# Batch 0's q and k: cast by GpSimd and transposed as bf16, with a new instruction order

## The chip, the cores and the metric

The kernel runs on one core of one Trainium2 chip. The metric is the device time of one execution in microseconds. The core has five engines that run side by side, each through its own list of instructions in order: TensorE (PE, with its weight loads shown apart as PEld), VectorE (DVE), ScalarE (ACT), GpSimd (POOL) and SyncE (SP), which here only issues DMAs. They wait for each other through semaphores.

## The reference

Eight batches, eight heads, 576 positions, head size 64. Linear attention with a feature map of 2 x 128 features, and then a gated linear unit with a causal convolution as gate:

```python
def phi(x):
    proj = np.einsum('bhsd,df->bhsf', x, w_phi)
    proj = proj - np.max(np.abs(proj), axis=-1, keepdims=True)
    return np.concatenate([np.exp(proj), np.exp(-proj)], axis=-1)
q_p, k_p = (phi(q), phi(k))
kv = np.einsum('bhsf,bhsd->bhfd', k_p, v)
z = np.sum(k_p, axis=2)
num = np.einsum('bhsf,bhfd->bhsd', q_p, kv)
den = np.einsum('bhsf,bhf->bhs', q_p, z)[..., None] + 1e-06
x = num / den            # then [batch, seq, heads * 64]
gate = sigmoid(causal convolution of x with conv_w, 5 taps)
out = (gate * (x @ w_val)) @ w_out
```

Inputs and output are fp32.

## The kernel before

Each batch goes through the same stages. q and k of a batch are seen as 18 blocks of 128 x 128; they are taken in five units `u` of 4, 4, 4, 4 and 2 blocks. Inside one batch:

- q and k are brought to SBUF and transposed to `qT` and `kT` (128 x 2304, bf16). For batches 2 to 7 a DMA transposes them (`xpose`). For batch 1 PE transposes bf16 data that a casting DMA has brought (`tp16`, evicted from PSUM by `tc16`). For batch 0 the fp32 data comes by nine plain loads of SyncE (`load32`: four pieces of k, five of q), PE transposes it as fp32 (`tp32`, L544) and DVE or ACT evicts it with a cast to bf16 (`tc32`, L550 and L552).
- `kp` and `qm` (L585) project a unit, 128 features by two row halves, into two PSUM banks. DVE takes the largest magnitudes (`kmax`, `qmax`, L593, tiles MK and MQP), ACT takes exp of plus and minus the projection of k (`kexp`, L603, tile KTIL).
- `ek` (ACT, L612) and `vs` (POOL, L618 and L619) scale v; `st` (PE, L628) sums k's features against v; `kv` evicts that (tile KV, by DVE at L636 or ACT at L640).
- The maxima of q are transposed and spread (`mqt`, `mqr`, `rx`: POOL at L690 or DVE at L693); `qp` (PE, L701 and L706) projects q again with the maxima taken off in the same banks; `qexp` (ACT, L714 and L717) gives QTIL and QTT.
- `num` (PE, L727 and L734), `nrm` (DVE, L745 and L748), `xtp` and `xtc` (transpose of x and its eviction), then `gate` (PE, L789), `tanh` (ACT, L793), `val` (PE, L799), `gv` (DVE, L805), `out` (PE, L821 and L825), `oev` (eviction) and `odma` (store).

The fp32 data of batch 0, `XN32`, lies in the memory of KTIL's second buffer, which batch 1's `kexp` writes. The three GV buffers are first written by `gv` of batches 0 to 2.

`build` writes all these steps as tasks with their dependencies. The order in which they are issued is a table, ORDER, of task numbers, found by a search outside the kernel; each engine runs its tasks in that order. FLEX names the engine of each task that may run on two, and BANKS the PSUM banks. The durations in the calls of `A(...)` served that search and issue nothing. WARM and ZERO are tables of filler for PE: `warm` multiplies ones by ones into a bank that is free (L499), `zero` adds products of zeros to a bank that has just been written (L512 and L505). In ZERO the entry `37:78:7` means: ahead of the 37th step, seven times, into the banks of task 78.

POOL also issues the casting loads of later batches' q and k. A tiny copy (`hold`, L517), which reads a piece of batch 0's q, stands ahead of batch 1's loads on POOL's queue, so that these do not start while batch 0's still run.

Of the kernel before, what the change touches and what calls it, by code (L numbers as in the profile page):

```python
# [14 lines left out]
BF16 = mybir.dt.bfloat16  # L15
# [19 lines left out]
WARM = "62:6:1 83:1:1 89:7:2 136:7:1 143:7:1"  # L35
ZERO = "37:78:7 63:82:5 77:36:1 103:107:1 120:101:1 128:217:8 146:225:1 157:194:4 160:202:1 177:317:6 191:348:1 197:243:2 199:243:2 213:329:1"
# [41 lines left out]
)  # L78
FLEX = (
    "DAAAAAADAAADDPPPPDDDDAADDDDDDDDDDDDDAAADAAAADDDDAAADDDAADAAADDADAADDDDADDDDADDDDDDAADADDAAAAAA"  # L80
)
BANKS = (
    "703736230700145452323232301670167671423236723010167601235442301014545450101366056467560145674501014545010167676701450145"
    "454567201237670123016767674567777356723236723234545230167232323236767454501545234362367010123234545445223014545016767676"
    "701012301450123016745012016736401234523674545455572301454523456723232301012323674523016723234670142201016745456701012165"
    "670145670101230167012301016723236767456702367726012323012323016746464450101670167012367674567234523234545012367015767234"
    "5010167452326322345670145670101674545012345012367452345010127452301014545670101765"
)


# [18 lines left out]
def dve(n, ov=0.075):  # L109
    return n / 960.0 + ov  # L110


def act(n):
    return n * 0.000833 + 0.067
# [794 lines left out]
```

## Time and profile before

| | |
|---|---|
| median of 3 runs | 218.67 us (217.57 to 219.39) |
| profiled execution, own time | 216.94 us |
| its span, first to last instruction | 215.2 us |
| instructions | 9031 |
| granted TensorE clock | 0.995 |
| PE busy / DVE / ACT / POOL | 195.4 / 170.0 / 180.5 / 132.9 us |

A page of the profile has the busy time of each engine, the span in 40 slices of 5.4 us with the busy share of each engine in tenths, the chain of work that ended last, and groups of instructions. A group's line reads: line of the kernel, engine, operation, what it writes and reads with the shapes, and count; then busy microseconds in total and the mean nanoseconds of one; then the idle time of that engine just before them and who ended it. In a timeline row stand the start, the length, the engine and the operation, and in brackets the idle time before it. "issue" as a releaser is time in which the engine waited for nothing that the profile shows. Matmuls overlap, so lengths of single ones add to more than their busy time.

### The profile page before, as it was taken

The page shows a single profiled execution, that of the slowest core. Times are in us where ns is not written, and L with a number is a line of the kernel's source. Part 1 is how long each engine was busy: PE and PEld are TensorE (multiplying, and loading weights), DVE is VectorE, ACT ScalarE, POOL GpSimd, SP SyncE. Part 2 cuts the span into 40 slices and gives each one's busy share as a digit, 9 for nine tenths or more (in the row PEclk, how much of TensorE's full clock was granted, in tenths as well). Part 3 has the DMA queues.
Part 4 walks back from the last instruction along what each step waited for, and adds up shares of the span by engine and source line. Part 5 has one row for each costly group of instructions (what it writes and reads, how often), then busy time and mean ns, then how long its engine had stood idle before and what let it go on. Part 6 is the DMA issues. An engine that isn't in the chain of part 4 may idle for free.

```text
span 215.2 us, 9031 instructions
## 1 busy us (share of the span) xinstructions
PE 195.4 (91%) x3948; PEld 138.4 (64%) x3948; DVE 170.0 (79%) x258; ACT 180.5 (84%) x267; POOL 132.9 (62%) x172
## 2 busy tenths in 40 slices
PE   2969788778999999999999999999999999999990
PEld 2745466566665776677767677568757766687640
DVE  3399789989599978999799978998699897654510
ACT  3799999999999899999899997999988988634351
POOL 3156999896893749953997099903992879210000
PEclk9999999999999999999999999999999999999997
DMA  6999989999999698969998978979953265773165
GB/s 195 371 223 199 297 175 192 231 195 198 138 241 251 113 172 241 264 104 188 216 303 155 116 146 259 187 154 202 280 179 84 67 160 128 97 165 88 49 205 188
DMA packets 49874, 39.89 MB, mean 185 GB/s; under 512 B 34149, under 2 KB 39461, under 8 KB 49834
## 3 DMA queue, kind: packets, MB, share of 16 engines
q1 hardware_dynamic: 43616, 28.65, 58.1%
q0 software_dynamic: 6032, 10.49, 26.5%
q8 instruction: 31, 0.51, 0.9%
q10 hardware_dynamic: 186, 0.17, 0.3%
q14 instruction: 9, 0.07, 0.1%
HBM read 30.45 MB, written 9.44 MB: 185 GB/s over the span
## 4 chain that ended last, share of the span: by engine, by line
PE 55%; ACT 22%; DVE 15%; issue 4%; DMA 1%; DVEq 0%; ACTq 0%
PE PS L799 11%; PE PS L821 10%; PE PS L789 9%; ACT QTIL L714 9%; ACT KTIL L603 9%; DVE MQP L593 5%; PE PS L727 5%; PE PS L585 4%; PE PS L628 4%; DVE MK L593 4%; PE PS L701 2%; PE PS L825 2%; PE PS L706 2%; PE PS L544 2%; DVE XN L748 2%
## 5 line engine op out<-in xcount | busy, mean ns | idle before, releaser
L603 ACT ACTIVATE KTIL<-PS 128x1024 bf16<-128x1024 f32 (+1 forms) x80 | 72.1, 965 | 4.0 <-PE PS L585 2.0
L618 POOL TENSOR_TENSOR VT<-VN,EK 128x1152 bf16<-128x1152 f32 x32 | 67.9, 2121 | 4.5 <-ACT EK L612 4.4
L714 ACT ACTIVATE QTIL<-PS 128x1024 bf16<-128x1024 f32 x64 | 62.6, 1047 | 2.3 <-PE PS L706 1.5
L690 POOL TENSOR_TENSOR RX<-MQR,ident 128x512 bf16<-128x512 bf16 (+1 forms) x39 | 36.6, 962 | 35.1 <-DVE MQR L678 32.4
L593 DVE TENSOR_REDUCE MK<-PS 128x8 f32<-128x1024 f32 (+1 forms) x40 | 44.3, 1113 | 3.4 <-PE PS L585 1.6
L593 DVE TENSOR_REDUCE MQP<-PS 128x8 bf16<-128x1024 f32 (+1 forms) x40 | 43.5, 1112 | 3.0 <-PE PS L585 2.3
L799 PE MATMUL PS<-XT,WV 128*128 128x288 bf16 x256 | 34.8, 286 | 0.2 <-DVE GV L805 0.2
L805 DVE SCALAR_TENSOR_TENSOR GV<-TH,PS 128x576 bf16<-128x576 bf16 x32 | 23.8, 752 | 10.4 <-PE PS L799 4.7
L821 PE MATMUL PS<-WOUT,GV 128*128 128x512 bf16 x128 | 31.3, 380 | 0.0
L799 PEld LDWEIGHTS <-WV 128*128 128x128 bf16 x256 | 23.8, 98 | 7.8 <-issue 1.4
L793 ACT ACTIVATE TH<-PS 128x576 bf16<-128x576 f32 x32 | 20.5, 667 | 8.8 <-PE PS L789 8.2
L789 PE MATMUL PS<-XT,GW 64*64 64x288 bf16 x640 | 23.6, 285 | 0.9 <-DVE RCP L745 0.4
L628 PE MATMUL PS<-VT,KTIL 64*128 64x65 bf16 x1152 | 23.1, 191 | 0.1
L748 DVE TENSOR_TENSOR XN<-PS,RCP 128x512 bf16<-128x512 f32 x32 | 22.1, 691 | 1.1
L727 PEld LDWEIGHTS <-QTIL 128*128 128x128 bf16 x512 | 18.3, 97 | 6.4 <-issue 4.1
L628 PEld LDWEIGHTS <-KTIL 64*128 64x128 bf16 x1152 | 20.7, 95 | 2.6 <-issue 1.5
L727 PE MATMUL PS<-KV,QTIL 128*128 128x65 bf16 x512 | 20.3, 193 | 0.3 <-DVE MQP L593 0.2
L789 PEld LDWEIGHTS <-GW 64*64 64x64 bf16 x640 | 18.0, 106 | 3.8 <-issue 1.6
L642 ACT ACTIVATE OUTS<-PS 128x512 f32<-128x512 f32 x22 | 13.7, 627 | 7.3 <-PE PS L821 6.1
L821 PEld LDWEIGHTS <-GV 128*128 128x128 bf16 x128 | 11.1, 98 | 11.3 <-issue 0.6
L585 PE MATMUL PS<-W,qT 64*128 64x128 bf16 x288 | 14.9, 217 | 3.8 <-ACT qT L552 0.9
L585 PEld LDWEIGHTS <-qT 64*128 64x128 bf16 x288 | 10.6, 94 | 10.4 <-issue 5.1
(82 smaller groups left out, 234.5 us busy)
## 6 DMA issues: line engine op xcount, KB each, us to landing
out_dram<-OUTS SPq DMA_DIRECT2D x32, 256.0 KB, 3.4
VN<-in_v_dram SPq DMA_DIRECT2D x7, 1152.0 KB, 7.2
KQN<-in_q_dram POOLq DMA_DIRECT2D x6, 576.0 KB, 8.0
KQN<-in_k_dram POOLq DMA_DIRECT2D x6, 576.0 KB, 9.1
KTIL<-in_k_dram SPq DMA_DIRECT2D x4, 288.0 KB, 3.7
VN<-in_v_dram POOLq DMA_DIRECT2D x1, 1152.0 KB, 12.3
KTIL<-in_q_dram SPq DMA_DIRECT2D x4, 256.0 KB, 4.9
out_dram<-OUTS SPq DMA_DIRECT2D x14, 64.0 KB, 2.4
```

The costliest lines, as they stand in the source:

```text
L585: nc.tensor.matmul(self.PS[:, t.grp.banks[par], i * P:(i + 1) * P], X[rows, (c0 + i) * P:(c0 + i + 1) * P], self.W2[rows, :], start=True, ...
L593: self.nc.vector.tensor_reduce(o, self.two(t.grp, n * P).rearrange("p a (c f) -> p a c f", f=F), AX.X, ALU.max, apply_absolute_value=True)
L603: self.nc.scalar.activation(self.KTIL[b % 2][:, s, c0:c0 + n, :, :].rearrange("p c a f -> p a c f"), self.two(t.grp, n * P).rearrange("p a ...
L618: nc.gpsimd.tensor_tensor(self.VT[g][:, s, :, 0:D], self.VN[b % 2][:, NC * g:NC * g + NC, :], e.to_broadcast([P, NC, D]), ALU.mult)
L628: nc.tensor.matmul(self.PS[:, t.grp.banks[ab], (s * 2 + x) * E1:(s * 2 + x + 1) * E1], self.KTIL[b % 2][rows, s, J // 2, J % 2, :], self.V ...
L690: self.nc.gpsimd.tensor_tensor(o, *wide(self.MQR[self.mq(b, u)][:, :], self.ident2), ALU.mult)
L714: self.nc.scalar.activation(o, i, AF.Exp, scale=1.0 - 2.0 * s)
L727: nc.tensor.matmul(self.PS[:, t.grp.banks[h // 4], (h % 4) * E1:(h % 4 + 1) * E1], Q[:, s, c % 2, h, (c // 2) * P:(c // 2 + 1) * P], self. ...
L748: nc.vector.tensor_tensor(o.rearrange("p (g h) d -> p g h d", g=ng), n[:, :, :, 0:D], rc.unsqueeze(3).to_broadcast([P, ng, 4, D]), ALU.mult)
L789: self.nc.tensor.matmul(self.PS[o * D:(o + 1) * D, t.grp.banks[par], 0:R], self.GW[r, jj, 4 - m, :], X[r, 4 * a + jj, :, HALO - 8 * s:HALO ...
L799: self.nc.tensor.matmul(self.PS[:, t.grp.banks[par], 0:R], self.WV[:, i, (2 * j + par) * D:(2 * j + par + 2) * D], X[:, 4 * par + i, :, HA ...
L821: nc.tensor.matmul(self.PS[:, t.grp.banks[0], :], GV[:, j, c % 2, (c // 2) * XH:(c // 2) * XH + P], self.WOUT[:, j, c % 2, :], start=(j == ...
```

## The change

Batch 0's q and k are no longer transposed as fp32. Per unit, a new task on POOL (`cast`) copies the fp32 columns to bf16, into `X16`, which lies in the first two GV buffers. PE transposes the bf16 columns (`tp0`) into a bank seen as bf16, and DVE or ACT evicts them (`tc0`). Batch 1's `kexp`, which overwrites the fp32 data, now depends on the casts and no more on the transposes. The first casts stand on POOL's queue ahead of `hold` and of the loads of batches 1 and 2.

ORDER, FLEX and BANKS are replaced whole by a new search; WARM goes from five entries with six products to two with three, ZERO from 14 entries with 41 calls to four with eight. In the new FLEX six of the ten evictions of batch 0's q and k are DVE's (all five of k, one of q), where one was; two of batch 1's small evictions go from DVE to ACT; of the 16 `kv` evictions ACT has eight, where it had four; of the 36 `oev` it has 19, where it had 22; of the 20 `xtc` three, where it had five; and the copy of the doubled weights W2 (`c_wd2`) goes from DVE to ACT. The nine loads on SyncE's queue were k0 k1 k2 q1 q0 q3 k3 q2 q4 and are k0 k1 q4 q1 k2 q0 k3 q3 q2. On POOL's queue the order at the start is cast k0, k1, q1, hold, cast k2, q0, k3, the four loads, cast k4, q2, q4, q3.

```diff
-WARM = "62:6:1 83:1:1 89:7:2 136:7:1 143:7:1"
-ZERO = "37:78:7 63:82:5 77:36:1 103:107:1 120:101:1 128:217:8 146:225:1 157:194:4 160:202:1 177:317:6 191:348:1 197:243:2 199:243:2 213:329:1"
+WARM = "70:0:1 207:6:2"
+ZERO = "137:227:2 141:196:4 223:339:1 259:335:1"
...
-                    tp = A("kp", b, u, "PE", 0.22 * n, fn("tp32", w, u), need, g, 0, rank=pr)
-                    h["x" + w, b, u] = A("kmax", b, u, ("DVE", "ACT"), (dve(n * P), act(n * P)), fn("tc32", w, u), [tp], g, rank=pr)
-                    h["tp", w, u] = tp
+                    ca = A("kp", b, u, "POOL", 0.1 + 0.14 * n, fn("cast", w, u), need, rank=pr)
+                    tp = A("kp", b, u, "PE", 0.06 * n, fn("tp0", w, u), [ca], g, 0, rank=pr)
+                    h["x" + w, b, u] = A("kmax", b, u, ("DVE", "ACT"), (dve(n * P), act(n * P)), fn("tc0", w, u), [tp], g, rank=pr)
+                    h.setdefault(("casts",), []).append(ca)
+                    h["tp", w, u] = ca
...
+        self.X16 = {w: self.GV[i][:, :, :, :].rearrange("p j a r -> p (j a r)") for i, w in enumerate("kq")}
...
-    def tp32(self, t, w, u):
+    def cast(self, t, w, u):
+        c0, n = UNITS[u]
+        sl = slice(c0 * P, (c0 + n) * P)
+        self.nc.gpsimd.tensor_copy(self.X16[w][:, sl], self.XN32[w][:, sl])
+
+    def tp0(self, t, w, u):
         c0, n = UNITS[u]
         for i in range(n):
-            self.nc.tensor.transpose(self.PS[:, t.grp.banks[0], i * P:(i + 1) * P], self.XN32[w][:, (c0 + i) * P:(c0 + i + 1) * P], self.ident_f[:, :])
-
-    def tc32(self, t, w, u):
+            self.nc.tensor.transpose(self.PS[:, t.grp.banks[0], :].bitcast(BF16)[:, i * P:(i + 1) * P],
+                                     self.X16[w][:, (c0 + i) * P:(c0 + i + 1) * P], self.ident[:, :])
+
+    def tc0(self, t, w, u):
         c0, n = UNITS[u]
-        o, i = self.XT_[w][0][:, c0 * P:(c0 + n) * P], self.PS[:, t.grp.banks[0], 0:n * P]
+        o, i = self.XT_[w][0][:, c0 * P:(c0 + n) * P], self.PS[:, t.grp.banks[0], :].bitcast(BF16)[:, 0:n * P]
```

More of the change, by code (lines that the diff above doesn't have):

```diff
@@ L41 @@
 ORDER = (
[36 rows of a table removed]
[36 rows of a table added]
 )
 FLEX = (
-    "DAAAAAADAAADDPPPPDDDDAADDDDDDDDDDDDDAAADAAAADDDDAAADDDAADAAADDADAADDDDADDDDADDDDDDAADADDAAAAAA"
+    "ADDDDDADAAAADPPPPDDDDADDADDADDADDDDDDAADAAADDDADDDAADDAADDADDDDDAAAAAAADDDDDADDDDDADAADAAAADDA"
 )
 BANKS = (
[L83 to L87, printed above, removed]
+    "612237661760145452323232367010167450423236723010167401234552345014545450101672447556470145674501014545010167676701450145"
+    "454567367236722323016767674523766646723236723230101234567670123236767454501545234364523014523454501502323014545016767016"
+    "701012301450167016723013230126745234523674545453463201454523016723232301012301674523010123232670141201450167456701235321"
+    "670145670101456767672345456723236767230120123456452367456723016725666450101670123676767454567672345234501452345016201454"
+    "5452323016723152345670101234567012345450167010145014501672315014523670123674562316"
 )
```

72 rows, old and new, of the table ORDER are left out of this document.

## The prediction

> **What bounds the kernel now.** I read the engine totals first, then the slices, then busy time by stage, then the chain of waits and the waits of ScalarE.
>
> ```profile
> PE 195.4 (91%) x3948; PEld 138.4 (64%) x3948; DVE 170.0 (79%) x258; ACT 180.5 (84%) x267; POOL 132.9 (62%) x172
> ...
> PE   2969788778999999999999999999999999999990
> ```
> ```profile
> 0.00:8.00 8.00, 4.20 (x31) 3.25 (x32) 1.86 (x7) 3.04 (x4) 1.94 (x12) 1.00 0.79 249
> 8.00:30.00 22.00, 17.89 (x284) 12.39 (x284) 19.28 (x25) 20.92 (x33) 15.32 (x17) 1.00 1.03 245
> 30.00:54.00 24.00, 19.20 (x547) 15.05 (x548) 22.83 (x34) 23.13 (x32) 20.87 (x24) 1.00 1.10 204
> 54.00:210.00 156.00, 154.05 (x3096) 107.70 (x3086) 126.07 (x195) 132.83 (x200) 94.76 (x120) 1.00 0.81 171
> ```
>
> After the length of each stretch, the columns are PE, PEld, DVE, ACT and POOL busy time. There are two regimes. From 54 to 210 us PE is busy 154.05 of 156.00 us: only 1.95 us can be found there by any order. From 8 to 54 us PE is busy 37.09 of 46, while ACT is busy 44.05, and so idle for only 1.95 us. DVE is busy 42.11 (3.89 idle) and POOL 36.19. So ScalarE, with DVE close behind, sets the pace of the front, and PE that of the rest. A microsecond won by ACT before 54 starts the PE-bound stretch a microsecond earlier; one won by PE alone in the front is worth nothing, except where the chain runs through it.
>
> PE's 37.09 us in the front is also less than it looks, since part of it is filler: zero products added to a finished bank (L512) and products of ones (L499).
>
> ```profile
> L544 PE MATMUL PS<-ident_f,KTIL 128*128 128x128 f32 x36 | 6.9, 334 | 4.1 <-DMA KTIL<-in_k_dram 3.8 <-DVE MQP L593 0.3
> L512 PE MATMUL PS<-ONES,NIL 64*128 64x128 bf16 (+1 forms) x150 | 6.7, 220 | 1.1 <-ACT QTIL L714 1.1
> L563 PE MATMUL PS<-ident,QTIL 128*128 128x128 bf16 x36 | 2.9, 220 | 0.0
> L499 PE MATMUL PS<-ONES 128*128 128x512 bf16 x6 | 2.1, 382 | 0.0
> ```
>
> These are PE's groups before 54 us: 8.8 us of filler, 6.9 us of fp32 transposes, and 2.9 us for as many bf16 transposes (those of batch 1).
>
> The start is a chain of its own (start, length, what):
>
> ```profile
> 0.74 2.93 DMA KTIL<-in_k_dram
> ...
> 3.80 1.09 PE PS L544 x4
> ...
> 5.13 1.90 PE PS L544 x8
> 7.03 0.97 PE PS L585 x16
> ```
>
> The first piece of k lands at 3.67. PE then takes 4.2 us for twelve fp32 transposes and two projections, so ScalarE's first exponential begins at 8.03:
>
> ```profile
> 4.92 0.58 ACT L552 CAST kT<-PS 128x512 bf16<-128x512 f32 x1 [1.53 <-PE PS L544]
> ...
> 8.03 1.94 ACT L603 ACTIVATE KTIL<-PS 128x1024 bf16<-128x1024 f32 x2 [0.39 <-PE PS L585]
> ```
>
> **The change, part by part.**
>
> *Start of the exponentials.* Now GpSimd casts 128x512, four bf16 transposes follow, DVE evicts, and the projection comes behind the second unit's transposes. No row shows a 128x512 cast on POOL. The nearest:
>
> ```profile
> L690 POOL TENSOR_TENSOR RX<-MQR,ident 128x512 bf16<-128x512 bf16 (+1 forms) x39 | 36.6, 962 | 35.1 <-DVE MQR L678 32.4
> L619 POOL CAST VT<-EK 128x18 bf16<-128x18 f32 x32 | 8.4, 262 | 0.0
> L776 POOL COPY XT<-XT 128x224 bf16<-128x224 bf16 x8 | 3.0, 373 | 13.1 <-DVE XT L636 7.2 <-ACT XT L640 5.9
> ```
>
> With 0.26 us for 18 columns and 0.37 for 224, the slope gives 0.53 for 512; the two-input product of that width, 0.96, is the upper end. I take 0.65, nearer the rows with one input. The Trainium skill (GPSIMD Engine Reference, Performance versus the Vector engine) has a tuned loop of 512 elements at 769 ns, a two-input add at about twice DVE's time; by it two casts in a row would give back an estimated 0.2 us of the start, which no run here shows yet.
>
> The DVE eviction reads bf16 from PSUM:
>
> ```profile
> L568 DVE COPY kT<-PS 128x1024 bf16<-128x1024 bf16 x2 | 1.4, 686 | 0.0
> L568 DVE COPY kT<-PS 128x256 bf16<-128x256 bf16 x1 | 0.3, 282 | 0.0
> L550 DVE CAST qT<-PS 128x512 bf16<-128x512 f32 x1 | 0.7, 691 | 3.3 <-PE PS L544 3.3
> ```
>
> 0.69 for 1024 columns and 0.28 for 256 put 512 at 0.42, against 0.69 for the fp32 form. So: land 3.67, cast to 4.4, transposes to 5.0, eviction to 5.45. The second piece was in use at 5.13 by the chain; cast to about 5.6, transposes to 6.0; the projection of the first unit (half of 0.97) to 6.5. The first exponential moves from 8.03 to about 6.5; with the bounds of the cast and of the second landing, 6.1 to 7.1.
>
> *ScalarE's list up to 54 us.* The earlier start isn't all gain, since ACT filled part of that wait with evictions. I count waits and work. Its waits before the first exponential were 8.03 less 3.04 busy, 5.0 us; now they are 6.5 less the table load of 1.28 and W2's small copy, also 5.0. So the gain is the change in work:
>
> ```profile
> L552 ACT CAST kT<-PS 128x512 bf16<-128x512 f32 x4 | 2.3, 584 | 2.5 <-PE PS L544 2.5
> L552 ACT CAST kT<-PS 128x256 bf16<-128x256 f32 x1 | 0.4, 407 | 0.0
> L640 ACT COPY XT<-PS 128x256 bf16<-128x256 bf16 x3 | 1.1, 377 | 0.9 <-PE PS L760 0.9
> L640 ACT CAST KV<-PS 128x520 bf16<-128x520 f32 x4 | 2.6, 647 | 0.0
> ```
>
> All five k evictions go to DVE: 4 x 0.584 + 0.407 = 2.74 us less. Two 256-column evictions of batch 1 come to ACT (2 x 0.377) and so does one KV eviction of batch 0 (0.647): 1.40 more. The net is 1.34 us less.
>
> *DVE.* Its first maximum and the W2 copy, which leaves it:
>
> ```profile
> 5.17 0.29 DVE L636 CAST W<-PS 128x128 bf16<-128x128 f32 x1 [0.97 <-PE PS L461]
> ...
> 9.41 2.35 DVE L593 TENSOR_REDUCE MK<-PS 128x8 f32<-128x1024 f32 x2
> ```
>
> It gains 4 x 0.42 + 0.28 for k, minus 0.27 for the q eviction that is now bf16, minus 2 x 0.28, minus 0.69 for KV (a row of that width, like the fp32 cast), minus 0.29 for W2: 0.15 us more. The first maximum can begin near 7 instead of 9.41, a gain of about 2.3 us. DVE isn't the bound of the front, though the four evictions stand among its maxima, so its wins by 20 us are smaller than 2.3.
>
> *GpSimd.* Eight casts of 0.65 and two of about 0.4 make 6.0 us, between 3.7 and 15, where it was idle:
>
> ```profile
> 9.95 0.19 POOL L517 CAST HOLD<-KTIL 128x1 bf16<-128x1 f32 x1 [7.41 <-DMA KTIL<-in_q_dram]
> 10.07 0.74 POOL L558 DMA_DIRECT2D QTIL<-in_q_dram  x1
> ...
> 15.48 1.04 POOL L690 TENSOR_TENSOR RX<-MQR,ident 128x512 bf16<-128x512 bf16 x1 [2.64 <-DVE MQR L675]
> ```
>
> Cover: 7.4 us of waiting before the hold and 2.6 us before the first RX product. On POOL's queue the four loads of batches 1 and 2 now stand behind the seventh of the nine loads (a k piece) and its cast, where they stood behind the ninth; the sum is an issue at 9 to 10.7 against 10.07: nothing, within 0.6 us. If the cover fails (the casts run into RX), the first q exponentials wait that long.
>
> *SyncE* issues the same nine loads with the 128-column-pair tail of q third; that holds up later pieces by about 0.4 us, which are not yet due.
>
> *Fillers.* 41 zero calls become 8 and six products of ones become three. Their PE time filled idle PE slots, except where the chain of waits of the front names L512, in five pieces of 1.81 us in all; the first and the last:
>
> ```profile
> 16.13 0.56 PE PS L512 x20
> ...
> 37.27 0.68 PE PS L512 x24
> ```
>
> I cost their removal at nothing, because ACT was busy beside nearly all of it; ACT's own waits on them are smaller, and I leave these for a rival:
>
> ```profile
> ACT QTIL L714 <- PE PS L512: 0.6, 2, 0.4
> ```
>
> *New waits.* Batch 1's small q eviction now stands on ACT ahead of batch 0's first q exponentials, so all of these wait for the load of q of batch 1 and its transposes. They are these:
>
> ```profile
> 19.44 0.61 PE L563 MATMUL PS<-ident,QTIL 128*128 128x128 bf16 x8
> ```
>
> They started at 19.44; ACT would get there at 18.5 to 19. Bounds 0 and 0.9 us; I take 0, as the load can start up to 1 us earlier.
>
> *The rest of the order.* In 54 to 210 us the bounds are a gain of the 1.95 us that PE idles, and a loss that no row bounds; I take zero. Over the whole kernel ACT loses two XT and three output evictions and gains four of KV; neither engine's total moves by over 3 us. The end is as long: before, an eviction and small stores behind the last matmul; now the same eviction and one larger store.
>
> The sum is -1.35 us on the profiled execution of 216.94 us (span 215.2), so 215.6 (span 213.9). The median of the three runs is 1.73 us higher, 218.67; the same shift gives **217.3 us**. A measurement of this kernel tells about 1%, 2.2 us, from no change.
>
> **The rivals.**
>
> *A, the front tightens more.* With the fillers gone from the chain and k ready earlier, ACT's 1.95 us of waiting between 8 and 54 goes too: 1.35 + 1.95 = 3.3 us, 215.4. For it: 0.6 us of those waits name a filler. Against: a search for a new order leaves new waits.
>
> *B, the new order idles PE later.* Every idle microsecond past 54 us costs one. It ends between 218.3 and 220.5, 219.5 as its middle, if PE idles 3.5 to 5 us there where it idled 1.95. For it: evictions of KV move to an ACT that is full in places:
>
> ```profile
> 80.00:90.00 10.00, 9.90 (x148) 6.49 (x146) 8.87 (x16) 10.00 (x17) 9.90 (x12) 1.00 1.09 262
> ```
>
> Against: ACT's whole list is shorter.
>
> *C, the slow clock lasts; slower.* The place is PE between 8 and 54 us. Matmul lengths show a slow clock at the start:
>
> ```profile
> 6.96 1.04 PE L585 MATMUL PS<-W,kT 64*128 64x128 bf16 x16
> ```
> ```profile
> 26.72 0.63 PE L585 MATMUL PS<-W,qT 64*128 64x128 bf16 x16
> ```
>
> The same sixteen products take 1.04 and later 0.63 us, 1.65 times as long; the change of pace comes at about 8.2, after 4.4 us of unbroken PE work. Now the first 4 us of PE work have gaps (casts and evictions between), and nearly all fillers are gone. If PE stays slow, the pieces of the front's chain that are PE work, without fillers and fp32 transposes, grow by 0.65 of themselves: from
>
> ```profile
> 15.73 0.40 PE PS L585 x8
> ...
> 53.36 0.20 PE PS L670 x2
> ```
>
> there are 20, 5.65 us in all, so +3.7 us: 217.3 + 3.7 = 221.0. It eats the whole gain from 2.1 us of slow chain pieces on, that is, if the slow pace lasts to about 22 us; to there alone the time is 218.7. The Trainium skill (TensorE: Matmul & The Clock Gate, The HAM clock gate) asks for a busy window of about 3.4 us before full rate and an idle one before the return; by that, sparse work may stay slow longer, but gaps under 3 us don't lose the pace. Its Part 4 adds that transposes don't count as busy; here the pace came after 4.4 us made up mostly of fp32 transposes, so this trace speaks against that.
>
> *D, no effect:* the casts or the second landing hold the first exponential at 8, and only ACT's list shrinks, given back by the wait for batch 1's q: 218.7.
>
> **How the numbers follow.** Forecast 0.36 (its own range 216.3 to 218.4), A 0.27, B 0.18, C 0.12, D 0.07. A and an edge of the forecast lie below 216.5: faster by over 1%, 0.32. C's upper half, and B where its idle is larger than I priced, lie above 220.9: 0.16. The rest is 0.52. The range runs from A, with 0.9 us of PE's idle beyond it, 214.5, to C, 221.0.
>
> **What would show it.** Right: the first KTIL exponential at 6.1 to 7.1; L603's and L552's rows with five evictions fewer; a POOL cast of 0.55 to 0.95; PE's full slices starting over a microsecond earlier; PE's idle past there under 3 us. Wrong: 64x128 groups of sixteen at 1 us beyond 10 us (C); ACT waits on batch 1's q near 19 us (D); PE idle of over 4 us behind 54 (B); ACT with almost no wait from 7 to 52 (A).

## The result and the profile after

The changed kernel takes 225.78 us (median of 4 runs, 224.72 to 227.28) where the kernel before takes 218.15 beside it: a ratio of 1.035 [1.027, 1.042]. It is slower by 7.6 us; 217.3 was forecast and 221.0 was the upper end of the range. The profiled run took 224.72 us, with a span of 222.9. Now and then a run of any kernel is slower as a whole; the times and ratios given from here on leave such runs out.

The page of the changed kernel, busy time of the engines and PE's slices:

```profile
PE 195.9 (88%) x3805; PEld 135.5 (61%) x3825; DVE 173.3 (78%) x261; ACT 178.7 (80%) x264; POOL 138.2 (62%) x182
...
PE   2889864889999999899999999989999999999990
```

Its busy time by stage, with the columns PE, PEld, DVE, ACT, POOL, granted clock:

```profile
0.00:8.00 8.00, 2.67 (x29) 1.89 (x30) 4.20 (x9) 3.07 (x4) 3.93 (x17) 1.00 0.76 240
8.00:30.00 22.00, 19.66 (x294) 13.22 (x292) 20.41 (x28) 19.89 (x33) 20.34 (x24) 1.00 1.11 250
30.00:54.00 24.00, 17.27 (x428) 12.73 (x425) 20.09 (x31) 22.64 (x32) 19.20 (x24) 0.93 0.95 186
54.00:210.00 156.00, 148.72 (x3037) 104.19 (x3047) 124.95 (x191) 130.12 (x193) 94.12 (x118) 1.00 0.76 162
210.00:218.00 8.00, 7.54 (x42) 3.45 (x41) 3.61 (x6) 2.75 (x5) 0.56 (x2) 1.00 0.71 226
```

The reader is to see three things. The engine totals have hardly moved: no engine has 7 us more work. Behind 54 us PE was busy for 154.05 of 156 us; now it is for 148.72, and its last matmul ends at 217.6 instead of 210.05. And in the front, 8 to 54 us, ACT is busy for 42.53 of 46 us (44.05 before): it is idle 1.5 us longer there than it was.

The start went as forecast. Timeline rows (start, length, instruction):

```profile
3.72 0.61 POOL L547 CAST GV<-KTIL 128x512 bf16<-128x512 f32 x1 [1.33 <-DMA KTIL<-in_k_dram]
...
5.83 1.08 PE L594 MATMUL PS<-W,kT 64*128 64x128 bf16 x16
...
6.48 3.77 ACT L612 ACTIVATE KTIL<-PS 128x1024 bf16<-128x1024 f32 x4 [1.41 <-PE PS L594]
```

The first exponential begins at 6.48 instead of 8.03. What is left of that at the end of the front is seen in the first four `gv` of DVE, which close batch 0 (count, then min/median/max length, first and last start). Before:

```profile
L805 DVE SCALAR_TENSOR_TENSOR GV<-TH,PS x4: 744/754/756, 57.9 to 65.5; 128x576 bf16<-128x576 bf16 x4
```

After:

```profile
L814 DVE SCALAR_TENSOR_TENSOR GV<-TH,PS x4: 742/754/755, 57.0 to 64.8; 128x576 bf16<-128x576 bf16 x4
```

The changed kernel is 0.9 us ahead at the first and 0.7 at the fourth. From there it loses 8 us, and not in one place: by the times of the same PE steps in the two traces (the median of those within 5 us; single steps differ by more, as their order differs) it is 1.2 us behind at 91 us, 3.6 at 135, 5.8 at 160 and 7.4 at 190. The waits of PE behind 54 us (who waited for whom: us in total, times, longest) say the same. Before, the view named three waits, of 0.8 us in all:

```profile
PE PS L789 <- DVE RCP L745: 0.4, 1, 0.4
PE PS L789 <- issue: 0.2, 1, 0.2
PE PS L799 <- DVE GV L805: 0.2, 1, 0.2
```

After, it names seventeen; the first two and some of the others:

```profile
PE PS L594 <- DVE XN L757: 0.7, 1, 0.7
PE PS L830 <- issue: 0.5, 3, 0.2
...
PE PS L637 <- POOL VT L628: 0.4, 1, 0.4
PE PS L736 <- DVE XT L645: 0.3, 1, 0.3
PE PS L808 <- DVE MQP L602: 0.3, 1, 0.3
...
PE PS L736 <- ACT KV L649: 0.3, 1, 0.3
```

They are short, and their releasers are steps of three engines. Not all of PE's idle time in this profile is real; the second line isn't a wait at all. The page above counts 3805 matmuls and 3825 weight loads: 20 matmul records are missing. Nineteen of them are of `out` (the other is a filler at 40 us); its group in the changed kernel, and then in a kernel with the same steps whose trace is whole (of the cut exponentials, below):

```profile
L830 PE MATMUL PS<-WOUT,GV 128*128 128x512 bf16 x109 | 29.7, 380 | 1.2 <-issue 0.5
```
```profile
L832 PE MATMUL PS<-WOUT,GV 128*128 128x512 bf16 x128 | 31.5, 380 | 0.0
```

The group lacks 1.8 us, but other products cover part of that in the count of PE's busy time. Put in where they must lie (the products of a step of `out` begin 0.216 us apart), the missing ones fill 1.0 us of idle time. From 54 us to the last matmul the changed kernel then idles 163.6 - 148.72 - 7.54 - 1.0 = 6.3 us, against 2.0 before. A whole trace of the same order, of the kernel with its clock held (below), has 6.3 as well:

```profile
54.00:219.40 165.40, 159.08 (x3126) 108.34 (x3117) 129.81 (x198) 133.97 (x202) 95.73 (x122) 1.00 0.76 165
```

That is 4.3 us of the loss; the other 3 must be in what counts as busy.

To find it I took the matmul records of the traces that are whole, in order, and cut PE's time over the last 262 steps (about 54 us to the end; they are the same steps in the old and the new order) in two: inside a step, from the start of its first product to that of its last, and between steps, from there to the first product of the next step. (The last product's own 0.4 us is in the first row only.) The time between steps is cut in three again: what the same kind of step takes in the median of the kernel before until a step of its own shape begins; 0.096 us for each change of shape, which is explained below; and the rest, which are waits. All in us:

| | before | new front, old rest | changed, clock held | changed, exponentials cut |
|---|---|---|---|---|
| last 262 steps of PE | 156.5 | 156.7 | 164.1 | 163.4 |
| inside the steps | 116.5 | 117.0 | 115.8 | 115.9 |
| between the steps | 39.7 | 39.3 | 48.0 | 47.1 |
| of these: to a step of the same shape | 26.7 | 26.7 | 26.7 | 26.7 |
| changes of shape | 9.8 | 9.8 | 12.1 | 12.1 |
| waits | 3.2 | 2.8 | 9.1 | 8.2 |
| steps whose shape differs from the step ahead | 102 | 102 | 126 | 126 |

Inside the steps PE runs as fast as before. The whole loss lies between them, and it has two parts. The larger is waits like those above, 5 to 6 us more than before; many are shorter than the view names, or than the modelled end of the product ahead of them. The other is a price of a certain succession of steps, seen in the timeline of the kernel before, in a stretch where PE never waits:

```profile
151.69 0.38 PE L706 MATMUL PS<-RX,ONES 64*128 64x512 bf16 x2
151.91 0.28 PE L585 MATMUL PS<-W,qT 64*128 64x128 bf16 x4
...
152.24 0.38 PE L706 MATMUL PS<-RX,ONES 64*128 64x512 bf16 x2
152.55 3.11 PE L799 MATMUL PS<-XT,WV 128*128 128x288 bf16 x24
...
155.61 0.61 PE L756 MATMUL PS<-ident,XN 128*128 128x128 bf16 x8
156.15 0.40 PE L585 MATMUL PS<-W,qT 64*128 64x128 bf16 x8
...
158.76 0.61 PE L756 MATMUL PS<-ident,XN 128*128 128x128 bf16 x8
159.21 1.03 PE L821 MATMUL PS<-WOUT,GV 128*128 128x512 bf16 x4
```

The same two products of L706 take 0.22 us until a step of their own shape (64*128) begins, and 0.31 until one of 128*128. The same eight transposes take 0.54 us to a step of 64*128 and 0.45 to one of 128*128. So a change of the shape in which the array is used costs some 0.09 us, and the page counts it as busy, because the modelled end of the last product covers it. Over the 262 steps of the kernel before, the median from the last product's start to the next step goes from 0.029 to 0.125 behind `num`, from 0.122 to 0.219 behind `val`, from 0.216 to 0.312 behind `out`, from 0.212 to 0.308 behind `qp`, and from 0.029 to 0.123 behind `st`: 0.09 to 0.10 each time. The Trainium skill (TensorEngine Tiling (Array Packing), Tiling Modes, Key Properties) says that a change of the tiling mode drains TensorE, and gives no figure; these traces agree and give one. The new order has 24 such changes more behind the front: 24 x 0.096 = 2.3 us at most. At 8 to 12 of them, by the trace, PE has a wait as well, which may hide the change; the others alone make 1.2 to 1.5 us.

### The profile page after: what moved, and what is told of

Same layout as the page of the kernel before. It is cut to its first block, busy times and chain, and to the rows that moved or that the text cites. A ratio compares the mean times of both kernels' runs of the same rounds, so it can differ in the third digit from the quotient of the medians.

```text
span 222.9 us, 8771 instructions
## 1 busy us (share of the span) xinstructions
PE 195.9 (88%) x3805; PEld 135.5 (61%) x3825; DVE 173.3 (78%) x261; ACT 178.7 (80%) x264; POOL 138.2 (62%) x182
## 4 chain that ended last, share of the span: by engine, by line
PE 59%; DVE 20%; ACT 10%; issue 5%; DMA 2%; POOL 1%; SPq 1%; DVEq 0%; ACTq 0%
PE PS L808 13%; PE PS L830 11%; DVE MQP L602 7%; PE PS L798 7%; PE PS L637 6%; PE PS L594 6%; ACT KTIL L612 5%; PE PS L736 4%; PE PS L710 3%; DVE MK L602 3%; DVE XN L757 3%; ACT QTIL L723 3%; PE PS L715 3%; DMA KTIL<-in_q_dram 2%; PE PS L834 2%
## 5 line engine op out<-in xcount | busy, mean ns | idle before, releaser
L808 PE MATMUL PS<-XT,WV 128*128 128x288 bf16 x256 | 35.5, 286 | 0.6 <-DVE MQP L602 0.3
L830 PE MATMUL PS<-WOUT,GV 128*128 128x512 bf16 x109 | 29.7, 380 | 1.2 <-issue 0.5
L798 PE MATMUL PS<-XT,GW 64*64 64x288 bf16 x640 | 24.2, 286 | 1.2 <-issue 0.5
L637 PE MATMUL PS<-VT,KTIL 64*128 64x65 bf16 x1152 | 21.9, 191 | 1.4 <-DVE XN L757 0.5
L637 PEld LDWEIGHTS <-KTIL 64*128 64x128 bf16 x1152 | 20.2, 95 | 4.7 <-DVE MQP L602 1.4
L651 ACT ACTIVATE OUTS<-PS 128x512 f32<-128x512 f32 x19 | 11.4, 601 | 11.5 <-PE PS L830 4.6
L594 PE MATMUL PS<-W,kT 64*128 64x128 bf16 x288 | 15.8, 228 | 3.3 <-ACT KV L649 1.1
L594 PE MATMUL PS<-W,qT 64*128 64x128 bf16 x288 | 16.4, 233 | 2.5 <-ACT KTIL L612 0.9
```

The source lines that it names most:

```text
L594: nc.tensor.matmul(self.PS[:, t.grp.banks[par], i * P:(i + 1) * P], X[rows, (c0 + i) * P:(c0 + i + 1) * P], self.W2[rows, :], start=True, ...
L637: nc.tensor.matmul(self.PS[:, t.grp.banks[ab], (s * 2 + x) * E1:(s * 2 + x + 1) * E1], self.KTIL[b % 2][rows, s, J // 2, J % 2, :], self.V ...
L798: self.nc.tensor.matmul(self.PS[o * D:(o + 1) * D, t.grp.banks[par], 0:R], self.GW[r, jj, 4 - m, :], X[r, 4 * a + jj, :, HALO - 8 * s:HALO ...
L808: self.nc.tensor.matmul(self.PS[:, t.grp.banks[par], 0:R], self.WV[:, i, (2 * j + par) * D:(2 * j + par + 2) * D], X[:, 4 * par + i, :, HA ...
L830: nc.tensor.matmul(self.PS[:, t.grp.banks[0], :], GV[:, j, c % 2, (c // 2) * XH:(c // 2) * XH + P], self.WOUT[:, j, c % 2, :], start=(j == ...
```

## The experiments

The tables can be taken apart. "Front" is the first 240 steps of the order (to about 48 us), "rest" all behind; ORDER, FLEX and BANKS are taken from the one search or the other, and a few banks at a seam are chosen anew where two uses would collide. Each ratio is to runs of the kernel before beside it.

**The casts alone, in the old order.**

```diff
-ORDER, FLEX, BANKS, WARM, ZERO = (the new search's)
+ORDER, FLEX, BANKS, WARM, ZERO = (before's, with each cast put in ahead of its transpose)
```

> The casts and bf16 transposes alone, with the order, engine and bank tables and the fillers of the kernel before (each cast is put just ahead of its transposes, the hold just ahead of batch 1's loads). Theory T (the new order loses time in the rest, 54 us on): the rest is as before, so 216 to 219 us, PE idle past 54 us under 2.5 us. Rival R (the casts themselves cost: a slow clock at the start, POOL's queue): 222 us or more, with 64x128 groups of sixteen at 1 us beyond 15 us.

Measured: 219.43, ratio 1.006 [1.002, 1.011], a little above the 216 to 219 expected. With the three last q casts put ahead of batch 2's loads, k's evictions on DVE, W2's copy on ACT and products of ones at the start:

```diff
-WARM = "71:6:1 93:1:1 ..."
+WARM = "3:6:9 9:6:1 18:6:3 32:2:2 72:6:1 93:1:1 ..."
```

> The casts with the old tables as before (219.6 us), the three last q casts put ahead of batch 2's loads, the evictions of k given to DVE, and products of ones ahead of the first data. If the casts' own gain of 1 to 2 us was eaten by the slow clock and by late casts, 215.5 to 217.5 us; if the front cannot give a gain to the rest, 218 to 220 us.

Measured: 218.64, ratio 1.002 [0.998, 1.006]. In the old order as it stands, the casts and the bf16 transposes lose 0.6%; with these moves they cost nothing that can be told. In neither case do they win anything by themselves.

**The fp32 transposes with the new tables.**

```diff
-    cast, tp0, tc0 with the new tables
+    tp32, tc32 with the new tables, the casts left out of them
```

> The new order, engine and bank tables and their few fillers, with the old fp32 transposes and no casts. Theory T: still slow, 223 to 228 us, PE idle past 54 us over 5 us. Rival R (the casts cost): near the kernel before, 217 to 220 us. Rival C (the slow clock in the front is the cost): the fp32 transposes flip the clock near 8 us, so 217 to 221 us.

Measured: 226.91, ratio 1.043 [1.037, 1.049]. The loss comes with the tables, with or without the casts.

**The new front with the old rest, and its mirror.**

```diff
-ORDER, FLEX, BANKS = (new)
+ORDER, FLEX, BANKS = (new for the first 240 steps, before's for all that are left)
```

> The changed kernel up to batch 0's transposes of x (240 steps, about 48 us), with its engines, banks and fillers; from there the order, engines and banks of the kernel before. Theory T (the new order loses time in the rest): PE idle past 54 us back under 2.5 us and 216 to 220 us. Rival F (what the new front leaves behind, slow clock included, is what it costs): 222 us or more.

Measured: 217.73, ratio 0.999 [0.996, 1.003]. The mirror:

```diff
+ORDER, FLEX, BANKS = (before's with the casts for the first part, new for all that are left)
```

> The mirror image: casts in the order of the kernel before, with its fillers, up to batch 0's transposes of x; from there the new order, engines and banks. Theory T: 223 to 227 us. Rival F: 218 to 220 us, like the casts with all the old tables (219.6).

Measured: 229.8, ratio 1.054 [1.046, 1.062]. That is 2.8 us above what was expected at most: the old front with the casts ends later too, and the last 262 steps begin at 57.1 us instead of 53.5. They take 156.7 us with the old rest behind the new front, and 164.8 with the new rest behind the old front; before, 156.5. So the length of the rest is that of its own table, whichever front runs ahead of it. And the front's 1.5 us are worth nothing to the old rest. Its first `gv`, in the kernel with the new front:

```profile
L815 DVE SCALAR_TENSOR_TENSOR GV<-TH,PS x4: 744/754/756, 58.1 to 65.7; 128x576 bf16<-128x576 bf16 x4
```

58.1 to 65.7, where it was 57.9 to 65.5: the lead has gone by then. One suspect was batch 1's `ek`, which the new front has 2 us later on ACT. It was moved ahead:

```diff
-... 175 240 80 211 327 122 328 210 123 245 358 436 437 329 126 359 438 441 216 ...
+... 175 240 80 216 211 327 122 328 210 123 245 358 436 437 329 126 359 438 441 ...
```

> The new front with the old rest (217.7 us), and batch 1's two EK exponentials moved on ScalarE's queue from behind batch 2's first exponential to behind batch 0's KV eviction, 2.5 to 4 us earlier. If EK (and with it the scaled v of batch 1 on GpSimd) is where the front's gain of 2 us is lost between 37 and 48 us: 215.5 to 217 us. If ScalarE's queue as a whole holds it back: 217 to 218.5 us.

Measured: 218.08, ratio 1.001 [0.997, 1.004]: no gain, so this was not the place.

**Half of the new order.**

```diff
+ORDER, FLEX, BANKS = (new up to the gates of batch 3, about 125 us, before's behind)
```

> The new order, engines and banks up to the gates of batch 3 (638 of 1074 steps, some 125 us), then those of the kernel before. If the loss is spread over the rest (small waits of PE all along): about half of it, 219.5 to 223 us. If it sits in one place early in the rest: 224 us or more; late in it: 218.5 us or less.

Measured: 222.61, ratio 1.021 [1.016, 1.027], 60% of the loss. PE by halves in this kernel (first number behind the length is PE busy):

```profile
54.00:130.00 76.00, 70.51 (x1523) 50.07 (x1522) 65.48 (x99) 66.68 (x97) 50.58 (x63) 1.00 0.93 191
130.00:215.00 85.00, 83.04 (x1542) 57.48 (x1545) 62.47 (x99) 64.58 (x99) 43.19 (x56) 1.00 0.62 147
```

It idles 5.5 us while the new table holds and 2.0 in the longer half where the old one does. This trace lacks 17 products of `out` behind 54 us; with these put in, and up to its last matmul, it is 5.1 and 1.4. It has 114 changes of shape in its rest, between 102 and 126. The loss is spread along the table.

**The engines of the rest alone, either way.**

```diff
+FLEX = (before's behind step 240; ORDER and BANKS new)
```

> The changed kernel; only behind its 240th step (some 48 us) each task that may run on two engines goes to the engine that the kernel before gave it; order, banks and fillers stay new. If the engines of the rest (eight KV evictions on ScalarE, more output and x evictions on DVE) are the cost: 220 us or less. If the order of the rest is: 223 us or more.

Measured: 228.99, ratio 1.051 [1.043, 1.058].

```diff
+FLEX = (the new one behind step 240; ORDER and BANKS before's)
```

> The new front, then the order and banks of the kernel before (217.7 us), but with the new engines in the rest. If the engines are the cost: 222 us or more. If the order is: 216.5 to 219.5 us.

Measured: 226.05, ratio 1.037 [1.031, 1.042]. The order of this last kernel's rest is the one that ran in 217.73; only the engine of some evictions differs, and PE now waits for these:

```profile
PE PS L638 <- DVE OUTS L648: 2.2, 1, 2.2
PE PS L766 <- ACT OUTS L652: 1.5, 1, 1.5
PE PS L766 <- DVE OUTS L648: 1.4, 1, 1.4
```

An eviction that changes its engine stands at a place in that engine's list which was not made for it, and PE waits for its bank. So order and engines are worth something only as a set, and what the new set loses can't be put down to its engines alone. ORDER and BANKS were exchanged together in every run, so that these two were not told apart.

**The clock.** TensorE's pace was rival C. In the changed kernel eight transposes show where it changes, and the rows of two stages, the slow start and a later one, follow (the granted clock is the number behind POOL's; the records begin only with the first change of pace, so that the slow start reads 1.00):

```profile
20.04 1.06 PE L572 MATMUL PS<-ident,QTIL 128*128 128x128 bf16 x8
...
23.24 0.62 PE L572 MATMUL PS<-ident,QTIL 128*128 128x128 bf16 x8
```
```profile
8.00:22.30 14.30, 13.07 (x129) 8.50 (x126) 13.01 (x21) 12.19 (x23) 12.64 (x18) 1.00 1.08 257
...
39.40:42.80 3.40, 3.04 (x37) 1.82 (x38) 1.90 (x4) 2.50 (x5) 2.23 (x2) 0.54 1.12 168
```

By the records of the granted clock it stays slow to 22.0 us, where it was slow to 8.2 before, and for another 3.4 us from 39.1 (the second row begins 0.3 us later, and so reads 0.54). Two kernels put filler back:

```diff
-WARM = "70:0:1 207:6:2"
+WARM = "15:3:9 70:0:1 207:6:2"
```

> The changed kernel with nine products of ones ahead of PE's first work, which run while PE waits for the first load. Theory C (the slow clock in the front is what it costs): full rate from about 6 us on, and 219 us or less. Theory T (the rest's order): the front ends 1 to 2 us earlier and the time is 223 to 225.5 us.

Measured: 224.66, ratio 1.033 [1.029, 1.037]; the pace rose at 7.4 us, and fell again from 10.8 to 21.0 and from 38.1 to 44.9.

```diff
-WARM = "70:0:1 207:6:2"
-ZERO = "137:227:2 141:196:4 223:339:1 259:335:1"
+WARM = "15:3:9 38:3:2 44:3:2 46:3:3 70:0:3 207:6:5"
+ZERO = "57:66:3 60:86:3 64:62:3 85:70:2 88:94:2 91:92:3 95:90:3 137:227:2 141:196:4 160:84:9 178:78:7 188:79:9 194:122:7 198:122:4 223:339:1 259:335:1"
```

> The changed kernel with fillers all through its front: products of ones before the first data and between the transposes, zero products behind the projections and at PE's waits between 31 and 40 us. Theory T: full rate from 7 us to the end, a gain of 1 to 3 us against 225 and still 222 to 224.5 us. Rival C (the clock is the cost): 220 us or less.

Measured: 226.69, ratio 1.040 [1.033, 1.048], at full rate from 6.4 us to the end of PE's work. Nothing comes back, where 222 to 224.5 was expected. In part this is the filler's own price, as the first `gv` now begins at 58.8 us instead of 57.0. But the last 262 steps, which run at full rate in either kernel, take 164.1 us here and 164.2 in the changed kernel: the slow clock isn't the cause of the loss. In the kernel before, on the other hand, the filler is worth its place:

```diff
-WARM, ZERO = (five and 14 entries)
+WARM, ZERO = "", ""
```

> The kernel before without any filler. Theory C: the clock falls to the slow state in the front, and the time rises by 3 us or more. Theory T alone, with the clock kept by real work: within 1% of 218 us, or 1 to 2 us faster as the fillers leave the chain.

Measured: 220.6, ratio 1.011 [1.005, 1.017], with two slow spells, at 18.8 to 22.2 and 39.3 to 42.7 us. That is some 2.4 us more, between what the two theories had.

**Late work, or the list?** PE's waits behind 54 us name steps of DVE and ACT. Either these engines have no slack there, or the new list puts a producer too close ahead of its consumer, however little else the engine has to do. The next six take work away from DVE, from ACT, and from both, in the changed kernel and in the kernel before: they leave out half of the maxima's columns, or half of the exponentials, of batches 2 to 7.

```diff
+        f1 = F if t.b < 2 else F // 2
-                self.two(t.grp, n * P).rearrange("p a (c f) -> p a c f", f=F),
+                self.two(t.grp, n * P).rearrange("p a (c f) -> p a c f", f=F)[:, :, :, 0:f1],
```

> The changed kernel, in which the key and query maxima of batches 2 to 7 read only the first half of each block of 128 features, so that VectorE has roughly 30 us less to do behind the front; the output is not the reference's. Nothing of TensorE's own list changes. Theory 1 (TensorE's idle time behind the front is time in which it waits for VectorE's results, which come late in the new order because VectorE has no slack there): idle time behind 54 us falls from 7.3 to 2 to 4 us and the time to 219 to 222. Theory 2 (TensorE's own list and its bank reuse are the cause, whatever VectorE does): time stays at 224 to 226. Theory 3 (ScalarE's results come late): at most 1.5 us less, 223.5 to 225.

> The same cut of the maxima of batches 2 to 7 in the kernel before (output not the reference's): the control. With 1.95 us of TensorE idle behind the front there is little to win: 216 to 218.5 under all three theories. A fall of over 3 us would say that VectorE's work costs TensorE time in some other way than by waits.

Measured: 222.87, ratio 1.025 [1.017, 1.032], above the 219 to 222 of a VectorE without slack, and for the control 216.64, ratio 0.997 [0.990, 1.003]. In the exponentials:

```diff
-            self.KTIL[b % 2][:, s, c0:c0 + n, :, :].rearrange("p c a f -> p a c f"),
+            self.KTIL[b % 2][:, s, c0:c0 + n, :, 0:f1].rearrange("p c a f -> p a c f"),
...
-            self.nc.scalar.activation(o, i, AF.Exp, scale=1.0 - 2.0 * s)
+            self.nc.scalar.activation(o[:, :, 0:h1], i[:, :, 0:h1, :], AF.Exp, scale=1.0 - 2.0 * s)
```

> The changed kernel, in which the key exponentials of batches 2 to 7 are made for the first 64 of each block of 128 features, and the query exponentials of the transposed form for half their columns, so that ScalarE has 15 to 25 us less to do behind the front; the output is not the reference's. Theory 3 (TensorE waits for ScalarE's late results): idle time behind 54 us falls from 7.3 to 2 to 4 us, time 219 to 222. Theory 1: at most 1.5 us less. Theory 2: no change, 224 to 226. If this and the cut of the maxima each win 2 to 3 us, both engines are without slack.

> The same cut of the exponentials of batches 2 to 7 in the kernel before (output not the reference's): the control. 216 to 218.5 under all theories.

Measured: 224.74, ratio 1.031 [1.026, 1.036], and 216.37, ratio 0.993 [0.988, 0.997]. With both cuts:

> The changed kernel with both cuts of batches 2 to 7 together (maxima over half of each block of features, exponentials of half; the output is not the reference's), so that VectorE has some 26 us and ScalarE some 40 us less to do behind the front. Theory 1+3 (TensorE waits for late work of both engines in turn, so that cutting one alone only hands the wait to the other): idle time behind 54 us falls to 2 to 4 us and the time to 218 to 221. Theory 2 (the waits come from the place of each producer and its consumer in the new list, whatever the engines' load): idle stays above 5 us, 222 to 225.

> Both cuts in the kernel before (output not the reference's): the control, 215 to 218 under each theory.

Measured: 221.75, ratio 1.015 [1.007, 1.022], and 215.71, ratio 0.988 [0.982, 0.994]. The busy time in the changed kernel with both cuts:

```profile
PE 194.3 (88%) x3805; PEld 135.0 (61%) x3825; DVE 146.7 (66%) x261; ACT 137.8 (62%) x264; POOL 138.3 (63%) x182
```

DVE has 27 us less to do and ACT 41, and the changed kernel is still 6.0 us slower than the kernel before with the same cuts; without cuts the distance was 7.6, with DVE's alone 6.2, with ACT's 8.4. The time, 221.75, lies between the ranges of the two theories. PE still idles 6.5 us behind 54 us (missing products put in), and 3.0 in the control; 1.9 and 1.3 of these are stalls inside one or two steps, for which the profile names no releaser. By the medians, then, 1.6 us of the 7.6 is late work. With the spread of four runs each it can be anything from nothing to over 4 us, and some 3.6 us of the distance stay at the least. What stays is in the tables: which step follows which, how close, and in which bank. Of the 7.6, the changes of shape are 1.2 to 2.3 us by their count; what remains are waits, 5 to 6 us by the gaps, whose places the runs did not single out. No run changed the number of shape changes and nothing else, so their price rests on the traces, not on an experiment. The profile of the run with VectorE's cut also has 3.2 us of waits for the transposing DMAs, so its idle time isn't used here.

No version that does the whole work beat the kernel before; the new front with the old rest equals it.

## Why the prediction was right or wrong

*Start of the exponentials:* right. Forecast 6.5, measured 6.48. The cast took 0.61 us (taken: 0.65, between 0.53 and 0.96), DVE's eviction 0.42 (0.42).

*ScalarE's list:* right in sign for the work, a little too large, and wrong in what follows from it. The evictions went and came as listed. But W2's copy, 0.27 us that came to ACT, was counted beside the waits and left out of the work, so that 1.35 should have been about 1.1. By 54 us ACT has done the same exponentials as before, and between 8 and 54 it was busy for 42.53 us instead of 44.05, as more of them lie ahead of 8; but its waits, which the step took as unchanged, rose. ACT's waits in that stretch, after; they had been 2.1 us:

```profile
ACT QTIL L723 <- PE PS L715: 1.3, 2, 0.9
ACT KTIL L612 <- PE PS L594: 1.2, 2, 1.0
ACT QTT L726 <- PE PS L715: 0.5, 1, 0.5
ACT TH L802 <- PE PS L798: 0.3, 1, 0.3
```

They are 3.3 us. The 0.9 us in the first row lies in the slow spell from 39.1 us. So of 1.35 us forecast 0.7 to 0.9 reached batch 0's `gv`.

*GpSimd, SyncE, batch 1's q:* right. The casts ended at 14.4, and RX still waited for 0.78 us behind them; the four loads were issued from 9.79 (10.07 before); batch 1's small q eviction began on ACT at 18.39 without a wait.

*Fillers at nothing:* wrong as a statement on the kernel before, where all of them together are worth 1.1%; right for the changed one, where putting them back won nothing.

*The rest of the order at zero:* this is the step that failed. It read PE's 154.05 us of busy time as work that any order must do, and so as a loss only what PE might idle more. It said itself that no row bounds this loss, and took zero, with the loss left to rival B. The rest took 164.2 us instead of 156.5: up to 2.3 us of it are changes of shape inside the busy time, and the larger part are waits, with 6.3 us of idle time instead of 2.0. Which of the new order, banks and engines brings the waits stays open, as they lose and win as a set.

*Rival B* had half of the mechanism, and was mis-sized. It priced 3.5 to 5 us of idle time; there were 6.3. (By its own sum its ends are 218.9 and 220.4, where it has 218.3 and 220.5.) With 6.3 the sum gives 217.3 + 6.3 - 1.95 = 221.7, not 225.8: much of the loss was not idle time in the profile at all, and B had no term for it. Its reason, the `kv` evictions on a full ACT, isn't borne out as the cause: cutting 40 us of ACT's work brought the two kernels no closer.

*Rival C:* its condition came true to the number, slow to 22.0 us, and its price did not: at full rate the kernel is no faster. *Rival A* and *D* fell with the result: the front did win, and by less than its forecast, not more.

The range missed because its upper end was C at 221.0, and nothing in it stood for an order that is worse everywhere by a little. A table of a thousand entries that is replaced whole is an unknown as large as any in the sum; the row to bound it by was the 40 us that PE spends between its steps. A count of the shapes in the old and new order, both known beforehand, would have shown up to 2.3 us of the loss; for the waits the prediction had no row.

## What to carry to other kernels

Where PE is the bound, count in its list how often the shape of the products changes: each change costs about 0.096 us where PE doesn't wait anyway, the profile shows it as busy, and an order with 24 more of them is up to 2.3 us longer at the same work. When an order, an engine table and a bank table are replaced together with a local edit, price the tables as a change of their own, and test them apart: here the edit won nothing and the tables cost 7.6 us. Before idle time is read off a trace, compare the counts of matmuls and weight loads; 20 missing records looked like 1.0 us of waiting.

## What the runs showed of the hardware that was not expected

- A change between 128*128, 128*64, 64*128 and 64*64 products costs 0.09 to 0.10 us on TensorE, behind each of the steps named above and in each of the twelve directions (in the kernel before, medians of 0.093 to 0.103).
- The pace of TensorE can stay slow for long while PE is busy most of the time. In the changed kernel PE was busy for 13.07 of the 14.3 us between 8 and 22.3, in short projections and bf16 transposes, and went to full rate only at 22.0. It came back to the slow rate for 3.4 us at 39.1 with no gap of PE over 1.14 us in the 4 us before, of which PE was busy for less than half. The Trainium skill (TensorE: Matmul & The Clock Gate, A second HAM failure mode) tells of a pace that goes to and fro through short idle times between groups of matmuls, and the trace agrees; its rule for keeping the pace, no idle gaps of PE over about 3 us (Why this matters for your kernels), was met here and didn't keep it.
- The pace changes on a fixed grid: in all 20 traces the time from one change of the granted clock to the next is a multiple of 3.41 us (in the changed kernel 17.06, 3.42 and 177.49), up to the end of PE's work. Full rate was lost 22 times ahead of that end, each time behind a stretch of 3.41 us in which PE was busy for 38 to 66%. Every stretch busy for less than 53% lost it, none of over 66% did, and in between both happened.
- A 128x512 cast from fp32 to bf16 takes 0.61 us on GpSimd, and 0.42 for 256 columns; VectorE moves a 128x512 bf16 bank out of PSUM in 0.42, ScalarE in 0.60.
